# Second pass of a channel-attention kernel: a planner's order replaced by a written list of steps

## The chip, the cores and the metric

One NeuronCore of a Trainium2 chip. The metric is the device time of one execution in microseconds, the median of three runs. Engines are named as in the profile: PE (TensorE, matmuls), DVE (VectorE), ACT (ScalarE), POOL (GpSimd) and SP (SyncE, which here only issues transfers). Each engine takes its own instructions strictly in the order in which the program holds them.

## The reference

```python
def reference(x, w1d):                       # x: 1 x 384 x 384 x 384, bf16; w1d: 1
    B, H, W, C = x.shape
    g = jnp.einsum("bhwc->bc", x) / (H * W)  # mean of every channel
    s = jax.nn.sigmoid(g * w1d[0])
    return x * s[:, None, None, :]           # each channel scaled by its own factor
```

The input has 147,456 positions of 384 channels (113 MB). All of it must be read before the first element of the output is known.

## The kernel before

**Tiling.** The positions are split over the 128 partitions. One *row* below is one position on each of the 128 partitions: 384 bf16 values or 768 bytes in a partition. There are 1152 rows. The SBUF array `arena` holds 275 of them; `arena[:, a : a + n, :]` is n rows from place a.

**First pass.** All 1152 rows are loaded, and PE adds them up with a matrix of ones (line 246). ACT turns the sum into the factors `s_bf` (line 433) and copies these to a PSUM bank (`s_ps`, line 437). 784 rows are *streamed*: summed and dropped. The other 368 are *kept*, so that they need not be loaded again: 72 as they are (raw rows), 296 *folded*, that is, four rows' bits are squeezed into the space of three, in ten groups. Group 0 has 16 rows, groups 1 to 8 have 32, and group 9 has 24 and one more. Groups 0, 1, 3, 5, 7 stand one above the other in the arena from place 12 on (the left column), groups 2, 4, 6, 8 from place 140 on (the right column); group 9 (`BANKED`) waits in PSUM banks.

**Second pass.** Every row is multiplied by the factors and stored. `scale` (line 446) does one multiplication of n rows on DVE or on POOL; `scale_both` gives the last rows of a piece to POOL and the others to DVE. Raw rows are scaled and stored at once. A group is unfolded in five steps (`unfold_rows`): `fields`, `signs` and `three` are bit operations on DVE (lines 280 and 286) that rebuild the fourth row, `threefold` scales three quarters of the group, and `fourth` scales the rest. As places come free, the 784 streamed rows are loaded again (line 240), scaled and stored (line 473).

**What sets the order.** `Flow.add` records each step with what it reads and writes; `Flow.emit` writes the instructions out in the order in which they were recorded, and adds a semaphore wait wherever a step needs another engine's result, or the end of a transfer. All loads and stores are issued by SP and use one queue, q1. Transfers count on 24 semaphores in turn, `f_SP0` to `f_SP23`. A wait on SP holds every transfer that stands behind it.

The order of the second pass comes from a planner in the kernel, which runs when the program is built. It advances a clock in steps of 0.05 and keeps lists of what has landed (`landed`), is unfolding (`turns`), waits for its store (`waiting`) and is in the queue (`moves`). It takes a row as 0.2267 us of transfer (`ROW`), a scaling as 0.15 + 0.2 us a row (`TT`), and decides by thresholds that change at set times (`BIG`, `CAP`, `PART`, `LOW`, `LAST`, `MERGE`, `DEEP`, `SHORT`, `PENDING`) when to load how many rows, and when to scale, unfold or store. POOL gets a fifth of a piece of ten rows or more (`share`). The groups come in the order 7, 8, 5, 6, 9, 3, 4, 1, 2, 0.

Of the kernel before, what the change touches and what calls it, by code (L numbers as in the profile page):

```python
# [131 lines left out]
def kernel(  # L132
# [319 lines left out]
    beside = [False]  # L452

    def share(n):
        return n // 5 if beside[0] and n >= 10 else 0

    def scale_both(a, n):

        m = share(n)
        before = [s for s in fl.steps[-40:] if s.eng == "DVE"][-1:]  # L460
        scale(a, n - m, s=s_ps if beside[0] else s_bf)
        if m:
            scale(a + n - m, m, "POOL", after=before)

    THIN = {raw(A): (0, 12, 13)}

    def store(chunk, a, lo, hi):
        r0, n = chunk
        cuts = THIN[lo] if chunk == KEPT and lo in THIN else (0, hi - lo)
        for i, j in zip(cuts, cuts[1:]):  # L470
            step = fl.add(
                "SP",
                lambda i=i, j=j: nc.sync.dma_start(  # L473
                    out=view(of, r0, n)[:, lo + i : lo + j, :], in_=arena[:, a + i : a + j, :]
                ),
                reads=rows(a + i, j - i), dma=True,
            )
        return step
# [14 lines left out]
    def unfold_rows(a, at, p, n, more):  # L493
# [26 lines left out]
        def threefold():  # L520
            scale_both(a, 3 * n)

        def fourth():

            bits(u, u, XOR, FIX, AND, 0xFFFF, uc, uc)
            scale(at, n + more, s=s_ps if beside[0] else s_bf)

        return [
            (fields, lambda: 2 * TS(n) + TT(n)),
            (signs, lambda: 2 * TS(n) + TT(n)),  # L530
            (three, lambda: TS(3 * n) + TT(n)),
            (threefold, lambda: SC(3 * n)),
            (fourth, lambda: TS(n) + TT(n + more)),
        ]

    def TS(n):
        return 0.15 + 0.1 * n

    def SC(n):
        return TT(n - share(n))  # L540

    def TT(n):
        return 0.15 + 0.2 * n

# [50 lines left out]
    written = []  # L595


    ROW, PER_LOAD, PER_STORE = 0.2267, 0.112, 0.061
    LAT, SEEN, DT = 0.4, 1.5, 0.05
    PENDING, MERGE = 24.0, 12.0  # L600
    BIG, CAP, PART, LOW, LAST = 32, 48, 16, 9.0, 4.0
    DEEP, SHORT = 6.5, 1.0
    BESIDE = True
    BANKS_AT = 2
    N_SPLIT = 2
    now = dve_at = 0.0
    moves, waiting, over, acts = deque(), deque(), deque(), deque()
    landed = deque()
    idle = [False] * ROWS
    todo = 0  # L610
    last_is_load = False

    def release(a, n):
        for i in range(a, a + n):
            idle[i] = True

    def runs():
        got, i = [], 0
        while i < ROWS:
            if idle[i]:  # L620
                j = i
                while j < ROWS and idle[j]:
                    j += 1
                got.append((j - i, i))
                i = j
            else:
                i += 1
        return got

    def send(chunk, a, lo, hi, then, known=None):  # L630

        waiting.append((dve_at, hi - lo, then, chunk, a, lo, [] if known is None else known))

    def backlog():
        return sum(e[1] for e in moves) + ROW * sum(e[1] for e in waiting)

    def split(n, m):
        k = -(-n // m)
        cuts = [n * i // k for i in range(k + 1)]
        return list(zip(cuts, cuts[1:]))  # L640


    SCRATCH = rows(Y, 8)
    needed = [set(SCRATCH + rows(U, 8)), set(SCRATCH + rows(V, 8)), set(SCRATCH)]

    def stored(a, n):

        def f():
            for i in range(a, a + n):
                for left in needed:  # L650
                    left.discard(("a", i))
                if not Y <= i < Y + 8 and not U <= i < U + 8 and not V <= i < V + 8:
                    idle[i] = True
        return f


    landed.append((STREAMED, LAST_ROW, N_STREAM, 1, True))
    for a, n in (
        (Y + 5, 2), (Y + 2, 3), (T + 7, 3), (T + 4, 3), (T, 4), (A + 26, 6), (A + 32, 7), (A + 13, 13), (V + 4, 4), (A, 13)
    ):  # L660
        landed.append((KEPT, a, raw(a), n, True))


    alongside = deque()
    t = 1.0
    for a, n in ((U, 4), (U + 4, 4), (V, 4)):
        scale(a, n, "POOL", after=[copied])
        t += 0.2 + 0.84 * n
        alongside.append((t, KEPT, a, raw(a), n))


    order = [g for i in (3, 2) for g in (1 + 2 * i, 2 + 2 * i)] + [BANKED]
    order += [g for i in (1, 0) for g in (1 + 2 * i, 2 + 2 * i)] + [FIRST]
    line = deque(order)
    home = {g: i for i, column in enumerate(COLUMNS) for g in column}
    home[BANKED] = 2
    free = [True, True, True]
    total = len(GROUPS)
    out_rows = 0
    turns = deque()  # L680
    bank_at = None
    since = None
    asked = checked = False
    stall = 0.0

    def start_group():

        if not line:
            return False
        g = line[0]  # L690
        column = home[g]
        if needed[column] or not free[column] or g == BANKED and (bank_at is None or now < bank_at[1]):
            return False
        line.popleft()
        free[column] = False
        a, q = GROUPS[g]
        if g == BANKED:
            a = bank_at[0]

        below = 0  # L700
        if column < 2 and g != COLUMNS[column][0]:
            below = GROUPS[COLUMNS[column][COLUMNS[column].index(g) - 1]][1]

        def part():
            release(a + below, sent - below)

        def done():
            nonlocal out_rows
            out_rows += 1
            free[column] = True  # L710
            release(a + max(below, sent), n_rows - max(below, sent))

        turns.extend(step + (None,) for step in unfold(g, a))
        sent, n_rows = 0, 4 * q + (g == BANKED)
        if len(line) >= total - N_SPLIT and q == PAIR:

            f, t, _ = turns[-2]
            sent = 3 * q
            turns[-2] = (f, t, lambda: send(KEPT, a, c_group[g], c_group[g] + sent, part, written))
        f, t, _ = turns[-1]  # L720
        turns[-1] = (f, t, lambda: send(KEPT, a + sent, c_group[g] + sent, c_group[g] + n_rows, done, written))
        return True

    held, sent_off, loads = None, 0, 0
    BEHIND = {9: 2, 10: 1, 14: 1, 15: 1}
    while True:
        if now > 25:
            BIG, CAP, PART, LOW, LAST = 64, 48, 24, 9, 4
            MERGE, DEEP, SHORT, PENDING = 5, 4, 0.5, 14
        if now > 80:  # L730
            BIG, CAP, PART, LOW, LAST = 24, 56, 32, 9, 1
            MERGE, DEEP, SHORT, PENDING = 5, 14, 0.5, 30
        if now > 150:
            BIG, CAP, PART, LOW, LAST = 56, 85, 12, 4, 3
            MERGE, DEEP, SHORT, PENDING = 12, 2, 2, 14
        if now > 200:
            BIG, CAP, PART, LOW, LAST = 32, 72, 16, 2, 1
            MERGE, DEEP, SHORT, PENDING = 3, 20, 3, 40
        if dve_at <= now:
            ahead = backlog()  # L740
            can = bool(turns)
            if not can and not alongside and (ahead >= PENDING or not landed):
                can = start_group()
            if landed and (ahead < PENDING or not can):
                chunk, a, lo, n, end = landed.popleft()
                beside[0] = BESIDE and not alongside and bool(line or turns)
                if beside[0]:
                    scale_both(a, n)
                else:
                    scale(a, n, s=s_ps if alongside and now else s_bf)  # L750
                dve_at = now + SC(n)
                since = (a, lo) if since is None else since
                if end or ahead < MERGE:
                    b, first = since
                    send(chunk, b, first, lo + n, stored(b, lo + n - first))
                    since = None
            elif can:
                f, t, then = turns.popleft()
                beside[0] = BESIDE and not alongside
                f()  # L760
                dve_at = now + t()
                if then:
                    then()
# [10 lines left out]
        if not asked and not line and not turns:  # L774
            verdict()
            asked = True
# [85 lines left out]
```

## Time and profile before

| | us |
|---|---|
| median of 3 runs | 718.23 |
| lowest and highest run | 718.22, 718.54 |
| span of the profiled execution, first to last instruction | 715.5 |
| PE, DVE, ACT, POOL busy in it | 211.7, 467.4, 116.5, 98.1 |
| factors ready (`s_bf` written) | about 268.0 |
| first store issued, last store issued | 268.5, 688.3 |

The profile shows one execution. Its page has the busy time of every engine, the span in 40 slices of 17.9 us, and groups of instructions by line. A group's row reads: line, engine, operation, output<-input, sizes (partitions x elements), xcount | busy us, mean ns of one | idle time ahead of them and what ended it. 384 elements are one row, so `128x1536` is a piece of four rows. In the rows by stretches the columns are: from:to, length, busy us of PE, weight loads, DVE, ACT and POOL, then the granted share of the PE clock, the share of the 16 DMA engines that were busy, and GB/s. A share can go a little over 1.00, since a packet is counted where it starts.

### The profile page before, as it was taken

How to read it: one execution, taken by the hardware profiler on the slowest of the kernel's cores; microseconds unless marked ns; L12 is line 12 of the kernel's file. 1: busy time of each engine (PE TensorE's matmuls, PEld its weight loads, DVE VectorE, ACT ScalarE, POOL GpSimd, SP SyncE). 2: the span in 40 equal slices, each digit the busy share in tenths (PEclk: the TensorE clock that was granted, in tenths of full speed). 3: DMA queues.
4: the chain of work that ended last, by engine and by line, in shares of the span. 5: the costliest groups of instructions: out<-in, count | busy, mean ns of one | idle time of the engine just before them, and what ended most of it. 6: DMA issues, size and time to landing. Idle time of an engine off the chain costs nothing.

```text
span 715.5 us, 2029 instructions
## 1 busy us (share of the span) xinstructions
PE 211.7 (30%) x1202; PEld 0.3 (0%) x3; DVE 467.4 (65%) x383; ACT 116.5 (16%) x97; POOL 98.1 (14%) x46
## 2 busy tenths in 40 slices
PE   5667967999598680000000000000000000000000
PEld 0000000000000000000000000000000000000000
DVE  4600001799989849999999999999940597007840
ACT  3700001476667630000110000000000000000000
POOL 0000000000000005414233431167100000000000
PEclk9899998999899995555555555555555555555555
DMA  9999999999999989999999999999999999999997
GB/s 382 428 447 419 439 431 428 452 416 433 426 431 426 429 351 379 405 412 433 430 431 437 438 422 440 434 438 437 440 418 453 420 444 439 419 439 440 439 417 338
DMA packets 15996, 303.68 MB, mean 424 GB/s; under 512 B 1778, under 2 KB 2418, under 8 KB 5106
## 3 DMA queue, kind: packets, MB, share of 16 engines
q1 hardware_dynamic: 15984, 303.57, 99.1%
q8 instruction: 4, 0.07, 0.0%
q14 instruction: 6, 0.05, 0.0%
q10 hardware_dynamic: 2, 0.00, 0.0%
HBM read 190.32 MB, written 113.25 MB: 424 GB/s over the span
## 4 chain that ended last, share of the span: by engine, by line
DMA 48%; DVE 29%; PE 16%; ACT 1%; issue 1%; DVEq 0%; SPq 0%; another core or an unknown queue 0%; POOLq 0%
DMA arena<-in_x_dram 37%; DVE arena L446 20%; PE bank L246 16%; DMA out_dram<-arena 12%; DVE arena L280 5%; DVE arena L286 4%; ACT arena L317 1%; DVEq L107 0%; SPq L473 0%; SPq L240 0%; ACT s_bf L433 0%; SPq L113 0%; SPq L857 0%; POOLq L107 0%
## 5 line engine op out<-in xcount | busy, mean ns | idle before, releaser
L246 PE MATMUL bank<-arena,ones 128*128 128x384 bf16 x1151 | 203.6, 341 | 47.0 <-DMA arena<-in_x_dram 46.9
L280 DVE TENSOR_SCALAR arena<-arena 128x1536 uint16<-128x1536 uint16 (+2 forms) x199 | 140.4, 750 | 105.7 <-DMA arena<-in_x_dram 98.8
L446 POOL TENSOR_TENSOR arena<-arena,s_bf 128x768 bf16<-128x768 bf16 (+3 forms) x42 | 97.9, 2336 | 426.3 <-ACT bank L437 268.0
L446 DVE TENSOR_TENSOR arena<-arena,bank 128x3072 bf16<-128x3072 bf16 (+13 forms) x61 | 138.0, 2304 | 4.3 <-DMA arena<-in_x_dram 3.6
L446 DVE TENSOR_TENSOR arena<-arena,s_bf 128x5376 bf16<-128x5376 bf16 (+4 forms) x27 | 76.5, 2901 | 95.1 <-DMA arena<-in_x_dram 84.9
L286 DVE TENSOR_TENSOR arena<-arena 128x3072 uint16<-128x3072 uint16 (+2 forms) x90 | 117.6, 1307 | 13.5 <-PE bank L246 10.7
L317 ACT ACTIVATE arena<-arena 128x3072 uint16<-128x3072 uint16 (+1 forms) x38 | 102.4, 2696 | 146.0 <-DVE arena L280 146.0
L563 PE MATMUL bank<-odd,ones 128*128 128x1 bf16 x1 | 0.2, 185 | 259.4 <-DVE odd L558 259.4
L384 ACT COPY arena<-bank 128x512 uint32<-128x512 uint32 (+2 forms) x8 | 4.2, 533 | 87.3 <-DMA out_dram<-arena 87.2
L246 PE MATMUL bank<-s_bf,ones 128*128 128x384 bf16 x48 | 8.3, 326 | 0.0
L317 ACT ACTIVATION_READ_ACCUMULATOR arena<-arena 128x1 f32 x38 | 7.1, 186 | 0.0
L384 ACT COPY bank<-arena 128x512 uint32<-128x512 uint32 (+2 forms) x8 | 3.8, 528 | 0.0
L260 PE MATMUL bank<-arena,ones 128*128 128x384 bf16 x1 | 0.5, 477 | 6.8 <-DMA arena<-in_x_dram 6.8
L433 ACT ACTIVATE s_bf<-bank,w_sc 128x384 bf16<-128x384 f32 x1 | 0.6, 581 | 9.5 <-PE bank L246 9.5
L830 ACT ACT_TABLE_LOAD x1 | 1.3, 1283 | 0.7 <-PEq L846 0.7
L337 DVE MEMSET ones<- 128x128 bf16 x1 | 0.2, 165 | 1.1 <-PEq L846 1.1
L342 PE MATMUL bank<-w_bf,ones 1*128 1x1 bf16 x1 | 0.2, 182 | 2.1 <-DMA w_bf<-in_w1d_dram 2.1
L347 DVE TENSOR_SCALAR w_sc<-bank 128x1 f32<-128x1 f32 x1 | 0.2, 158 | 0.9 <-PE bank L342 0.9
L567 DVE CAST odd_i<-bank 128x1 int32<-128x1 f32 x1 | 0.2, 159 | 0.3 <-PE bank L563 0.3
L437 ACT COPY bank<-s_bf 128x192 uint32<-128x192 uint32 x1 | 0.3, 322 | 0.0
L563 PEld LDWEIGHTS bank<-odd,ones 128*128 128x128 bf16 x1 | 0.1, 103 | 517.7 <-DVE odd L558 517.7
L384 ACT COPY arena<-rest 128x64 uint32<-128x64 uint32 x1 | 0.2, 244 | 0.0
(10 smaller groups left out, 1.4 us busy)
## 6 DMA issues: line engine op xcount, KB each, us to landing
arena<-in_x_dram SPq DMA_DIRECT2D x3, 6912.0 KB, 36.2
out_dram<-arena SPq DMA_DIRECT2D x3, 6912.0 KB, 28.4
arena<-in_x_dram SPq DMA_DIRECT2D x4, 4608.0 KB, 24.5
arena<-in_x_dram SPq DMA_DIRECT2D x6, 3072.0 KB, 19.6
out_dram<-arena SPq DMA_DIRECT2D x6, 3072.0 KB, 21.6
arena<-in_x_dram SPq DMA_DIRECT2D x2, 6144.0 KB, 31.5
arena<-in_x_dram SPq DMA_DIRECT2D x2, 4992.0 KB, 23.1
arena<-in_x_dram SPq DMA_DIRECT2D x1, 8160.0 KB, 26.5
```

Of the source, the lines that this page charges most:

```text
L246: return pe.add_instruction(mybir.InstMatmult(name=nc.get_next_instruction_name(), ins=[pe.lower_ap(rhs), pe.lower_ap(ones[:])], outs=[pe. ...
L260: return nc.tensor.matmul(acc, lhsT=ones[:], rhs=arena[:, i, :], start=first, stop=last)
L280: lambda: nc.vector.tensor_scalar(out=dst, in0=src, scalar1=s0, scalar2=s1, op0=op0, op1=op1),
L286: "DVE", lambda: nc.vector.tensor_tensor(out=dst, in0=a, in1=b, op=op), reads=reads, writes=writes
L317: lambda: nc.scalar.activation(out=y, in_=y, func=ACTF.Copy, accum_out=seen[:, 2 * k + i : 2 * k + i + 1]),
L337: fl.add("DVE", lambda: nc.vector.memset(ones[:], 1.0), writes=["ones"])
L384: "ACT", lambda: nc.scalar.copy(dst.bitcast(u32), src.bitcast(u32)), reads=reads, writes=writes
L433: lambda: nc.scalar.activation(out=s_bf[:], in_=acc, func=ACTF.Sigmoid, scale=w_sc[:, 0:1]),
L437: "ACT", lambda: nc.scalar.copy(s_ps.bitcast(u32), s_bf[:].bitcast(u32)), reads=["s_bf"], writes=["bank0"]
L446: lambda: vec.tensor_tensor(out=v, in0=v, in1=s[:, None, :].to_broadcast([P, n, C]), op=Op.mult),
L563: lambda: nc.tensor.matmul(votes, lhsT=ones[:], rhs=odd[:], start=True, stop=True),
L830: nc.scalar.preload_act_table(ACTF.Sigmoid)
```

## The change

The planner with its clock, thresholds and lists is taken out. In its place stands `PLAN2`, a list of 164 entries, which a short loop turns into steps:

- `("M", a, n, m)`: scale n rows from place a, the last m of them on POOL
- `("U", g, a, m)`: the next unfolding step of group g, which stands at place a; in `threefold`, m rows go to POOL
- `("L", a, n)`: load the next n streamed rows to place a
- `("W", a, n)`: store n rows from place a
- `("B", a)`: bring group 9 back from the PSUM banks

The groups now come in the order 7, 5, 3, 8, 6, 1, 4, 2, 9, 0, and each piece has its own number of rows for POOL. The two passes' sums, the bit operations and the numbers of rows are the same. The diff, cut to its core:

```diff
-    def share(n):
-        return n // 5 if beside[0] and n >= 10 else 0
-
-    def scale_both(a, n):
-        m = share(n)
+    def scale_both(a, n, m):
         before = [s for s in fl.steps[-40:] if s.eng == "DVE"][-1:]
-        scale(a, n - m, s=s_ps if beside[0] else s_bf)
+        scale(a, n - m, s=s_ps if folded[0] else s_bf)
         if m:
             scale(a + n - m, m, "POOL", after=before)
...
-    def store(chunk, a, lo, hi):
+    def store(a, n):
+        chunk, lo = where[a]
...
-    ROW, PER_LOAD, PER_STORE = 0.2267, 0.112, 0.061
-    BIG, CAP, PART, LOW, LAST = 32, 48, 16, 9.0, 4.0
...
-    while True:
-        if now > 25:
-            BIG, CAP, PART, LOW, LAST = 64, 48, 24, 9, 4
...
+    PLAN2 = [
+        ("M", 274, 1, 0), ("M", 259, 4, 0), ("W", 274, 1), ("M", 269, 3, 0), ("W", 259, 4), ("M", 263, 3, 0),
...
+        ("U", 7, 84, 0), ("W", 246, 6), ("W", 232, 1), ("W", 216, 4), ("L", 252, 15), ("U", 7, 84, 0), ("L", 220, 32),
...
+    todo, turns = 0, {}
+    for kind, a, *more in PLAN2:
+        if kind == "M":
+            n, m = more
+            if a == LAST_ROW:
+                scale(a, n)
+            else:
+                scale_both(a, n, m)
+        elif kind == "W":
+            store(a, *more)
+        elif kind == "L":
+            (n,) = more
+            load(STREAMED, a, todo, todo + n)
...
+        else:
+            first, m = more
...
+            step = turns[a].popleft()
+            if step.__name__ == "threefold":
+                step(m)
+            else:
+                step()
```

In the rows below, a transfer is `DMA output<-input`, its size is partitions x elements, and the brackets name the semaphores that the instruction waits for: `f_DVE` and `f_POOL` count those engines' steps, `f_SP` and a number the end of a transfer.

SP at the start of the second pass, up to its first load. Before:

```order
L473 DMA out_dram<-arena 128x384 [waits f_DVE]
L473 DMA out_dram<-arena 128x768 [waits f_DVE]
L473 DMA out_dram<-arena 128x1152 [waits f_DVE] x3
L473 DMA out_dram<-arena 128x1536 [waits f_DVE]
L473 DMA out_dram<-arena 128x1536 [waits f_POOL]
```

Now:

```order
L467 DMA out_dram<-arena 128x384 [waits f_DVE]
L467 DMA out_dram<-arena 128x1536 [waits f_DVE]
L467 DMA out_dram<-arena 128x1152 [waits f_DVE] x2
L467 DMA out_dram<-arena 128x768 [waits f_DVE]
L467 DMA out_dram<-arena 128x1536 [waits f_POOL]
L467 DMA out_dram<-arena 128x2688 [waits f_DVE]
```

The second store has four rows instead of two.

SP around the first loads of the second pass. Before:

```order
L473 DMA out_dram<-arena 128x4608 [waits f_DVE]
L473 DMA out_dram<-arena 128x384
L240 DMA arena<-in_x_dram 128x8064 [waits f_SP23,f_SP0,f_SP22,f_SP2,f_SP3]
L240 DMA arena<-in_x_dram 128x4992 [waits f_SP5]
L240 DMA arena<-in_x_dram 128x4992 [waits f_SP8,f_SP9]
```

Now:

```order
L467 DMA out_dram<-arena 128x4608 [waits f_DVE]
L467 DMA out_dram<-arena 128x2304 [waits f_DVE,f_POOL]
L467 DMA out_dram<-arena 128x384 [waits f_DVE]
L467 DMA out_dram<-arena 128x1536 [waits f_DVE,f_POOL]
L240 DMA arena<-in_x_dram 128x5760 [waits f_SP22,f_SP20,f_SP1,f_SP2]
L240 DMA arena<-in_x_dram 128x12288 [waits f_SP6,f_SP4,f_SP7,f_SP8]
L467 DMA out_dram<-arena 128x5760 [waits f_DVE,f_POOL]
L467 DMA out_dram<-arena 128x9216 [waits f_DVE,f_POOL]
L467 DMA out_dram<-arena 128x3072 [waits f_DVE]
L240 DMA arena<-in_x_dram 128x4608 [waits f_SP12]
L467 DMA out_dram<-arena 128x12288 [waits f_DVE,f_POOL]
L467 DMA out_dram<-arena 128x4608 [waits f_DVE,f_POOL]
```

Loads of 15 and 32 rows stand in place of 21, 13 and 13. Two stores ahead of them now wait for POOL too, and a load of 12 rows with its store follows.

POOL at the start of the second pass, its first pieces. Before:

```order
L446 TENSOR_TENSOR arena<-arena,s_bf 128x1536 [waits f_ACT]
L446 TENSOR_TENSOR arena<-arena,s_bf 128x1536 x2
L446 TENSOR_TENSOR arena<-arena,s_bf 128x768 [waits f_DVE,f_SP10]
L446 TENSOR_TENSOR arena<-arena,s_bf 128x768 [waits f_DVE]
L446 TENSOR_TENSOR arena<-arena,s_bf 128x768 [waits f_DVE,f_SP11]
```

Now:

```order
L446 TENSOR_TENSOR arena<-arena,s_bf 128x1536 [waits f_ACT]
L446 TENSOR_TENSOR arena<-arena,s_bf 128x1536 x2
L446 TENSOR_TENSOR arena<-arena,s_bf 128x1152 [waits f_DVE]
L446 TENSOR_TENSOR arena<-arena,s_bf 128x768 [waits f_DVE]
L446 TENSOR_TENSOR arena<-arena,s_bf 128x1152 [waits f_DVE,f_SP10]
```

Pieces of three and two rows, which wait for DVE but for no load, stand ahead of the first piece that waits for a load.

264 lines of the change are left out of this document (40 added, 224 removed), and 26 rows, old and new, of the table PLAN2.

## The prediction

> **What bounds the kernel now.** I read the page's slices and DMA queues first, because they say in a few lines whether transfers ever pause.
>
> ```profile
> span 715.5 us, 2029 instructions
> PE 211.7 (30%) x1202; PEld 0.3 (0%) x3; DVE 467.4 (65%) x383; ACT 116.5 (16%) x97; POOL 98.1 (14%) x46
> ...
> DMA  9999999999999989999999999999999999999997
> ...
> q1 hardware_dynamic: 15984, 303.57, 99.1%
> ...
> HBM read 190.32 MB, written 113.25 MB: 424 GB/s over the span
> ```
>
> No compute engine passes 65%, while queue q1 (all of SP's transfers) keeps the 16 DMA engines at work for 99.1% of the span. Only slice 15 (from 250 us on) and the last one are below 9. The chain of waits gives VectorE 29% of the end, which misleads here: it follows semaphores, and a store that waits for a scaling may still find a long queue ahead of it. So I then asked for stretches of the second pass, which starts at 267.5 us, when the scale is ready.
>
> ```profile
> 266.00:270.00 4.00, 1.42 (x9) 0.00 (x0) 1.93 (x4) 0.90 (x2) 1.52 (x1) 1.00 0.14 49
> 270.00:285.00 15.00, 0.00 (x0) 0.00 (x0) 14.93 (x12) 0.00 (x0) 7.69 (x3) 0.51 1.02 416
> 285.00:290.00 5.00, 0.00 (x0) 0.00 (x0) 4.90 (x4) 0.00 (x0) 0.00 (x0) 0.50 1.03 364
> 290.00:295.00 5.00, 0.00 (x0) 0.00 (x0) 4.16 (x4) 0.00 (x0) 1.64 (x1) 0.50 0.97 413
> 295.00:300.00 5.00, 0.00 (x0) 0.00 (x0) 5.00 (x3) 0.00 (x0) 4.14 (x3) 0.50 1.00 387
> ...
> 315.00:320.00 5.00, 0.00 (x0) 0.00 (x0) 4.97 (x4) 0.00 (x0) 0.23 (x1) 0.50 0.97 372
> 320.00:530.00 210.00, 0.18 (x1) 0.10 (x1) 202.09 (x130) 4.41 (x9) 78.82 (x34) 0.50 1.01 434
> 530.00:710.00 180.00, 0.00 (x0) 0.00 (x0) 76.15 (x26) 0.00 (x0) 0.00 (x0) 0.50 1.00 434
> 710.00:716.00 6.00, 0.00 (x0) 0.00 (x0) 0.00 (x0) 0.00 (x0) 0.00 (x0) 0.50 0.17 73
> ```
>
> The last two columns are the share of the DMA engines and GB/s. From 270 to 710 us the share is 0.97 to 1.03: transfers never pause. The rate is 434 GB/s for 390 us and lower only early (364, 387, 372) though the share is full there: packets take longer, the queue isn't empty. VectorE is nearly as full until 527 us, but nothing is won by making it less so.
>
> A row of all 128 partitions is 128 x 768 B = 98,304 B, so at 434 GB/s it takes 0.2265 us. The second pass moves 784 rows in and 1152 out (bytes read, less the first pass's 1152 rows, plus bytes written: 190.3 MB), 438.5 us at that rate. From the first store's bytes (a little after 269 us) to about 711.5 us it takes 442. Some 3.7 us are all that a better order could recover; what it can lose is not bounded.
>
> **The change part by part.** The same code and the same order run up to the scale; 784 rows are still loaded and 1152 stored. What moves is the order behind 268 us, so I price four things: the head, the number of transfers, the places where the queue could run dry, and the slow early packets.
>
> *The head.* The first store (1 row) is as before. The second needs a scaling of 4 rows where it needed 2.
>
> ```profile
> L446 DVE TENSOR_TENSOR arena<-arena,bank 128x1536 bf16<-128x1536 bf16 x4 | 3.8, 951 | 0.1
> L446 DVE TENSOR_TENSOR arena<-arena,bank 128x1152 bf16<-128x1152 bf16 x4 | 2.8, 750 | 0.1
> L446 DVE TENSOR_TENSOR arena<-arena,bank 128x768 bf16<-128x768 bf16 x1 | 0.6, 555 | 0.0
> ...
> 269.00:270.00 1.00, 0.00 (x0) 0.00 (x0) 1.00 (x2) 0.00 (x0) 1.00 (x1) 1.00 0.42 146
> ```
>
> Before, the queue waits 0.555 - 0.23 = 0.33 us for the second store and 0.75 - 0.45 = 0.30 for the third. Now it waits 0.95 - 0.23 = 0.72 for the second and not at all for the third, 0.75 against 0.91 us of transfer. That is +0.1 us; bounds 0 and +0.4 (the whole 951 - 555 ns).
>
> *Number of transfers.* 46 stores replace 48, the loads stay 20. A transfer's own cost isn't shown; it lies between nothing and the 0.33 us that SP takes to issue one.
>
> ```profile
> L473 SPq DMA_DIRECT2D out_dram<-arena x48: 332/333/1252, 268.5 to 688.3; - x48
> ...
> DMA to landing us min/median/max: 1.6/15.7/39.6
> ```
>
> So 0 to -0.7 us. I take -0.1, near nothing: SP's issuing runs beside full transfers.
>
> *Cover.* The queue runs dry if a store or load reaches it after what is ahead has gone. SP issues in its order, so each wait also holds all that stand behind. I need VectorE's and GpSimd's durations:
>
> ```profile
> L446 POOL TENSOR_TENSOR arena<-arena,s_bf 128x1152 bf16<-128x1152 bf16 x2 | 4.7, 2370 | 2.4 <-DMA arena<-in_x_dram 2.4
> L446 POOL TENSOR_TENSOR arena<-arena,s_bf 128x768 bf16<-128x768 bf16 x22 | 36.0, 1640 | 50.3 <-DVE arena L286 26.7 <-DMA arena<-in_x_dram 15.5 <-DVE arena L446 7.9
> ...
> L286 DVE TENSOR_TENSOR arena<-arena 128x3072 uint16<-128x3072 uint16 x24 | 42.1, 1756 | 0.6
> L446 DVE TENSOR_TENSOR arena<-arena,bank 128x7680 bf16<-128x7680 bf16 x10 | 41.4, 4148 | 0.9 <-DMA arena<-in_x_dram 0.9
> L280 DVE TENSOR_SCALAR arena<-arena 128x3072 uint16<-128x3072 uint16 x40 | 37.5, 955 | 0.5
> ...
> L446 DVE TENSOR_TENSOR arena<-arena,bank 128x3072 bf16<-128x3072 bf16 x14 | 24.4, 1752 | 1.1 <-DMA arena<-in_x_dram 0.8
> L280 DVE TENSOR_SCALAR arena<-arena 128x9216 uint16<-128x9216 uint16 x8 | 20.5, 2559 | 0.2
> ```
>
> Scaling on VectorE costs (4.148 - 1.752) / 12 = 0.20 us a row and 0.15 fixed; unfolding steps one and two cost 2 x 0.955 + 1.756 = 3.67 us each, step three 2.56 + 1.76 = 4.3. A store's bytes follow its issue by about 1 us (first issue 268.5, bytes in 269 to 270), and I allow 2.5 us between the first DMA engine's end and the last one's (estimate: the share falls after 710 us while the span runs to 715.5).
>
> First place: both first loads stand behind a store that waits for GpSimd.
>
> ```profile
> 268.48 9.21 POOL L446 TENSOR_TENSOR arena<-arena,s_bf 128x1536 bf16<-128x1536 bf16 x3 [268.03 <-ACT bank L437]
> ...
> 268.07 12.70 DVE arena L446 x11
> ```
>
> GpSimd's three opening pieces end at 277.7 as before. VectorE's 12.70 us for 11 scalings of 59 rows become 10.3 for the 9 scalings of 48 rows up to the 12-row one, at 278.4. Then GpSimd's new pieces of 3 and 2 rows run to 278.4 + 2.37 + 1.64 = 282.4, SP issues the 4-row store, then the 15-row load, whose bytes can start at 283.9. Ahead of that store stand 67 rows, 269.3 + 0.7 + 15.2 = 285.2 us. It arrives at 283.4: 1.8 us of cover, cost nothing. Before, the first load was issued at 282.6 behind 74 rows; about the same.
>
> Second: the 12-row store behind the 12-row load. Behind that load stand 32 rows to store, 7.2 us. Spread 2.5, scaling of 10 rows 2.15, issue 1.0: 1.6 us are left.
>
> Third: the 19-row store, ahead of which VectorE does three unfolding steps of the next group (11.7 us) and scales 30 rows in three pieces (6.5), GpSimd then 3 rows (2.4); with the issue 21.6 us. When the 47-row load ahead of it is issued, 19 + 21 + 47 rows are queued, and a 32-row store follows: 27 us, less 2.5. Some 3 us are left, if VectorE starts that group when the load is issued.
>
> Later stores have transfers of 32 to 74 rows ahead (7 to 17 us). At the end the 74-row store has the 55-row load and the 47-row store ahead (23 us) against 15.1 us of scaling: 8, less 3.5. So starving costs 0, with bounds 0 and +4 (2.5 us more lag would overrun the first two places by some 1 us each, stores between them by as much).
>
> *The slow early packets.* Against 434 GB/s the stretches at 285, 295 and 315 us lose 0.81 + 0.54 + 0.71 = 2.06 us. They lie where small loads and stores alternate, and these are what the list rearranges: now 15 and 32 rows in, 15, 24 and 8 out, 12 in, 32 out, for 21, 13, 13 in and 10, 11, 13, 24 out. The profile doesn't name their cause. Bounds: none left, -2.06; twice as many, +2.06. I take the same loss: the alternation stays.
>
> Sum: 718.2 + 0.1 - 0.1 + 0 + 0 = 718.2 us. The profiled span is 715.5, the runs' median 718.23; the 2.7 us between are taken as they are.
>
> **A rule against it.** In the trace GpSimd's pieces ran beside VectorE's scalings from PSUM alone; while VectorE unfolds, GpSimd is idle (285 to 290 us: VectorE 4.90, GpSimd 0.00). Now the 3- and 2-row pieces run to 282.4 while unfolding starts at 280. The Trainium skill (SBUF — State Buffer, Who interferes with whom) says that a VectorE instruction in a 2-port mode, or with two SBUF inputs, and a GpSimd one exclude each other: the later fully blocks until the first is done. By that rule alone the 2-row piece could start one VectorE instruction late, at most 1.76 us by the row above, and the sum stays 718.2. No row here shows the two side by side.
>
> **Rivals.** *The early loss shrinks* (faster): with larger first transfers packets run at 434 GB/s, 718.2 - 2.06 = 716.2 at best; to be seen it must give back 1.4 of the 2.06. For it: those stretches alone are slow, and all small. Against: loads and stores still alternate there.
>
> *The cover is too thin* (slower): landings are seen, or VectorE is ready, some 2 to 3 us later than worked out; then the 12-row store, and the 15- and 24-row ones before it, reach an empty queue. From 1.6 us on, each us costs one, and at two or three places: +1.5 to +4, 720 to 722. For it: covers of 1.6 to 3 us on clocks carried over 15 to 110 us. Against: the present order has equally thin places (its first load), and shares of 0.97 and more.
>
> *GpSimd is kept out until unfolding pauses* (slower): its 2-row piece starts only after three steps, 280.0 + 11.7 = 291.7, ends at 293.3; store and loads reach a queue that emptied at 285.2, near 294.3: +9, 727 us. It decides from 1.8 us of delay. For it: nothing ran so before. Against: gaps between VectorE's instructions let GpSimd in.
>
> **How the numbers follow.** No change, early loss as now: 0.55, 718.2, own range 717.0 to 719.6. Early loss shrinks: 0.18, near 716.5. Thin cover: 0.19, near 721. GpSimd kept out: 0.08, 720 to 727. A difference is told from 0.2%, 1.44 us: faster below 716.8, 0.18; within, 0.55; slower above 719.7, 0.27. The range 716.3 to 721.8 leaves out GpSimd's bad case and some of both others.
>
> **What would show it.** Right: share 0.97 or more in every stretch from 271 to 710 us, first load issued near 283, GpSimd's 2-row piece ended near 282.5, 12-row store with bytes waiting ahead. Wrong: a dip of the share at 285, 298, 319 or 388 us; a GpSimd piece much over 0.73 us a row (2.37 for 3); or 285 to 320 us at 430 GB/s throughout (faster), or lower than now (slower).

## The result, and the profile after

The changed kernel takes 721.22 us (median of 7 runs, 719.93 to 722.74) against 718.28 us for the kernel before on the same chip (7 runs, 717.99 to 719.77). The ratio is 1.0037, 95% interval 1.0025 to 1.0048: slower, by 2.7 us. The forecast was no change, 718.2 us; the time lies inside its range, at the upper end, but above the 717.0 to 719.6 us that it gave to no change. The profiled execution took 721.69 us with a span of 719.5.

The page after, in the rows that answer to those of before:

```profile
PE 215.4 (30%) x1202; PEld 0.3 (0%) x3; DVE 475.3 (66%) x359; ACT 116.6 (16%) x97; POOL 90.1 (13%) x38
...
DMA  9999999999999989999999999999999999999997
...
q1 hardware_dynamic: 15696, 303.57, 98.9%
...
L280 DVE TENSOR_SCALAR arena<-arena 128x1536 uint16<-128x1536 uint16 (+2 forms) x199 | 147.8, 788 | 114.8 <-DMA arena<-in_x_dram 97.5
```

At this resolution nothing has happened: queue q1 is at 98.9% instead of 99.1%, and slices of 18 us average the loss away. One row is odd: the bit operations of line 280 have the same count and shapes as before and yet take 788 ns on average, where they took 750. The row before:

```profile
L280 DVE TENSOR_SCALAR arena<-arena 128x1536 uint16<-128x1536 uint16 (+2 forms) x199 | 140.4, 750 | 105.7 <-DMA arena<-in_x_dram 98.8
```

The loss shows in stretches of 5 to 25 us, whose last two columns are the share of the DMA engines that were busy and GB/s. After:

```profile
285.00:290.00 5.00, 0.00 (x0) 0.00 (x0) 4.90 (x4) 0.00 (x0) 0.00 (x0) 0.50 0.91 287
290.00:295.00 5.00, 0.00 (x0) 0.00 (x0) 4.82 (x4) 0.00 (x0) 0.44 (x1) 0.50 1.07 432
295.00:300.00 5.00, 0.00 (x0) 0.00 (x0) 5.00 (x2) 0.00 (x0) 4.78 (x2) 0.50 0.94 405
...
390.00:395.00 5.00, 0.00 (x0) 0.00 (x0) 4.97 (x3) 0.00 (x0) 1.25 (x2) 0.50 0.86 368
...
415.00:420.00 5.00, 0.00 (x0) 0.00 (x0) 4.93 (x4) 0.00 (x0) 0.00 (x0) 0.50 1.08 415
...
445.00:450.00 5.00, 0.00 (x0) 0.00 (x0) 5.00 (x2) 0.00 (x0) 2.37 (x1) 0.50 1.02 368
...
530.00:710.00 180.00, 0.18 (x1) 0.10 (x1) 113.85 (x58) 0.51 (x2) 13.48 (x6) 0.50 1.00 434
```

The same view of the kernel before, at the three later places:

```profile
390.00:395.00 5.00, 0.00 (x0) 0.00 (x0) 4.37 (x2) 0.00 (x0) 3.23 (x2) 0.50 1.02 437
415.00:420.00 5.00, 0.00 (x0) 0.00 (x0) 4.96 (x4) 0.00 (x0) 3.10 (x1) 0.50 0.99 428
445.00:450.00 5.00, 0.00 (x0) 0.00 (x0) 5.00 (x3) 0.00 (x0) 1.76 (x1) 0.50 1.02 437
```

Two kinds of loss are to be told apart. At 285 and 390 us the *share* falls (0.91, 0.86): the queue ran dry. At 415 and 445 us the share is full (1.08, 1.02) and only the *rate* is low (415 for 428, 368 for 437): there is work, but packets take longer. From 530 us on all is as before, 434 GB/s.

Rows of 5 us are rough: a packet is counted where it starts, and in the kernel before the share goes from 0.82 to 1.21 between 480 and 700 us though its engines are busy throughout. The trace also has a record of every packet, and two sums over these are used below, in us for each of the 16 DMA engines. *Idle time* is time without a packet. *Slow packets* are the time of each packet above the shortest of its size in these profiles. Idle time is 0.75 us from 280 to 300 us and 0.47 from 380 to 400, against 0.08 and 0.02 before.

The sums account for the loss. From its first packet to its last, the second pass of these two executions takes 448.0 us for 444.5. Of the 3.5 us, 2.2 are slow packets (4.9 us for 2.7; 1.6 for 0.1 of them from 390 to 460 us), 1.5 are idle time, and 0.3 came back because there are fewer packets.

The timeline of the changed kernel (start, duration, engine, line; the number in brackets is idle time and what ended it) shows what came late, at the first place and at the third:

```profile
279.06 4.67 POOL L446 TENSOR_TENSOR arena<-arena,s_bf 128x1152 bf16<-128x1152 bf16 x2 [0.82 <-DVE arena L446]
280.29 4.25 DVE L280 TENSOR_SCALAR arena<-arena 128x3072 uint16<-128x3072 uint16 x2
284.51 2.66 SPq L240 DMA_DIRECT2D arena<-in_x_dram  x2
...
366.24 0.33 SPq L240 DMA_DIRECT2D arena<-in_x_dram  x1
368.41 1.82 DVE L280 TENSOR_SCALAR arena<-arena 128x3072 uint16<-128x3072 uint16 x2
...
375.95 2.36 POOL L446 TENSOR_TENSOR arena<-arena,s_bf 128x1152 bf16<-128x1152 bf16 x1 [11.01 <-DVE arena L280]
376.39 4.34 DVE L280 TENSOR_SCALAR arena<-arena 128x9216 uint16<-128x9216 uint16 x1
...
390.40 0.34 SPq L467 DMA_DIRECT2D out_dram<-arena  x1
```

At both places a GpSimd piece runs beside a bit operation, and the bit operation stretches: two 8-row operations take 4.25 us at 280.29 and 1.82 at 368.41, where GpSimd is idle; the 24-row operation takes 4.34 where it took 2.56 before. At the third place SP issues the 19-row store only at 390.40. In the trace's records of transfers, the 32-row store ahead of it was through on the first of the 16 DMA engines at 390.45 and on the last at 393.30; the new store's packets begin at 391.25, and until then the faster engines had nothing to do. The time from the first to the last of the 16 engines to finish one transfer, 2.85 us here, is called the *lag* below.

### The profile page after: what moved, and what is told of

It reads as the page before. It is cut to its first block, busy times and chain, and to the rows that moved or that the text cites. A ratio compares the mean times of both kernels' runs of the same rounds, so it can differ in the third digit from the quotient of the medians.

```text
span 719.5 us, 1992 instructions
## 1 busy us (share of the span) xinstructions
PE 215.4 (30%) x1202; PEld 0.3 (0%) x3; DVE 475.3 (66%) x359; ACT 116.6 (16%) x97; POOL 90.1 (13%) x38
## 3 DMA queue, kind: packets, MB, share of 16 engines
q1 hardware_dynamic: 15696, 303.57, 98.9%
## 4 chain that ended last, share of the span: by engine, by line
DMA 50%; DVE 28%; PE 15%; ACT 2%; DVEq 1%; POOL 1%; issue 1%; SPq 0%; POOLq 0%
DMA arena<-in_x_dram 37%; DVE arena L446 16%; PE bank L246 15%; DMA out_dram<-arena 12%; DVE arena L280 7%; DVE arena L286 5%; ACT arena L317 2%; DVEq L107 1%; POOL arena L446 1%; SPq L240 0%; SPq L467 0%; ACT s_bf L433 0%; SPq L113 0%; SPq L683 0%; POOLq L107 0%
## 5 line engine op out<-in xcount | busy, mean ns | idle before, releaser
L280 DVE TENSOR_SCALAR arena<-arena 128x1536 uint16<-128x1536 uint16 (+2 forms) x199 | 147.8, 788 | 114.8 <-DMA arena<-in_x_dram 97.5
L246 PE MATMUL bank<-arena,ones 128*128 128x384 bf16 x1151 | 207.5, 345 | 43.7 <-DMA arena<-in_x_dram 43.5
L446 DVE TENSOR_TENSOR arena<-arena,bank 128x3072 bf16<-128x3072 bf16 (+24 forms) x54 | 155.2, 2912 | 27.2 <-DMA arena<-in_x_dram 26.7
L446 POOL TENSOR_TENSOR arena<-arena,s_bf 128x1536 bf16<-128x1536 bf16 (+6 forms) x34 | 89.9, 2648 | 492.3 <-ACT bank L437 268.6
L446 DVE TENSOR_TENSOR arena<-arena,s_bf 128x9984 bf16<-128x9984 bf16 (+7 forms) x10 | 59.4, 5994 | 57.5 <-DMA arena<-in_x_dram 46.8
L260 PE MATMUL bank<-arena,ones 128*128 128x384 bf16 x1 | 0.5, 477 | 6.9 <-DMA arena<-in_x_dram 6.9
```

Source lines behind the costliest of these rows:

```text
L246: return pe.add_instruction(mybir.InstMatmult(name=nc.get_next_instruction_name(), ins=[pe.lower_ap(rhs), pe.lower_ap(ones[:])], outs=[pe. ...
L260: return nc.tensor.matmul(acc, lhsT=ones[:], rhs=arena[:, i, :], start=first, stop=last)
L280: lambda: nc.vector.tensor_scalar(out=dst, in0=src, scalar1=s0, scalar2=s1, op0=op0, op1=op1),
L446: lambda: vec.tensor_tensor(out=v, in0=v, in1=s[:, None, :].to_broadcast([P, n, C]), op=Op.mult),
```

## The experiments

The measured times below stand beside a run of the kernel before on the same chip; "ratio" is against that. All edits are to the list `PLAN2` of the changed kernel, but for one. The questions in order: is it the stretched bit operations, is it the first pieces, is it the addresses, is it the dry queue at 390 us, and what do 415 and 445 us have to do with that?

**The kernel before, unchanged (c_before).**

> The kernel before, unchanged, as a measure of what runs of one kernel differ by: ratio 1.000 within 0.002. Its profile shows how much of the second pass's length (444.5 us in the first profile, 448.0 in the changed kernel's) is the order's own: within 0.7 us of 444.5 if the slow packets belong to the order, up to 447 if they come and go by chance.

718.45 us (12 runs), ratio 0.9999, 0.9989 to 1.0009. Its second pass takes 445.0 us for 444.5 and has 2.4 us of slow packets for 2.7, so these belong to the order. A ratio of 1.001 can't be told from 1 here, one of 1.002 can.

**No GpSimd piece beside the first unfolding (e1_start).** The pieces of 3 and 2 rows go to VectorE:

```diff
-("M", 246, 6, 3), ("W", 220, 12), ("M", 232, 1, 0), ("M", 216, 4, 2),
+("M", 246, 6, 0), ("W", 220, 12), ("M", 232, 1, 0), ("M", 216, 4, 0),
```

> The two GpSimd pieces of 3 and 2 rows that ran to 283.7 us beside unfolding are given to VectorE. Theory lock (GpSimd and VectorE's unfolding hold each other up, so the 4-row store and the first loads came late): the two bit operations at 280 us take 1.9 us again instead of 4.25, the first load is issued at about 282.5 instead of 284.5, the share at 285 to 290 us is 1.00 instead of 0.91, and about 1.0 us is won against the changed kernel: near 720.2. Theory size (the slow packets belong to the small transfers and loads of 15 and 32 rows, whoever scales): share 1.00 but the rate at 285 to 290 stays under 370 GB/s, win 0.5 at most: 720.7.

Its timeline, and its stretch at 285 us:

```profile
280.58 1.82 DVE L280 TENSOR_SCALAR arena<-arena 128x3072 uint16<-128x3072 uint16 x2
...
283.16 3.42 SPq L240 DMA_DIRECT2D arena<-in_x_dram  x2
```

```profile
285.00:290.00 5.00, 0.00 (x0) 0.00 (x0) 4.90 (x4) 0.00 (x0) 0.00 (x0) 0.50 1.00 367
```

The lock is confirmed: the two bit operations take 1.82 us instead of 4.25. The first load is issued 1.35 us earlier, though 0.70 of that is only an earlier start of this execution's second pass (first store at 268.30 for 269.00). Idle time from 280 to 300 us falls from 0.75 to 0.24. The rate stays at 367 GB/s, as the size theory had it. The whole time doesn't move: 721.17 us, ratio 1.0044 (1.0022 to 1.0065). The gap at 285 us is real, and no gain from closing it can be seen; in this profile the idle time at 380 to 400 us is 1.28 us for 0.47, which hides half a microsecond.

**No GpSimd piece beside the unfolding at 376 us (e2_mid), and beside none at all (e3_all).**

```diff
-("M", 68, 6, 3),
+("M", 68, 6, 0),
```

> The 3-row GpSimd piece at 376 us, which ran beside a bit operation of 24 rows (4.34 us instead of 2.56), goes to VectorE. Theory lock: the 19-row store is issued some 1.2 us earlier than at 390.4 (1.8 less 0.6 for three more rows), the share at 390 to 395 us rises from 0.86 to 0.95 or more, and if a queue that runs dry brings the 16 DMA engines into step and makes packets slow afterwards (theory step), the slow stretches at 415 and 445 us go too: 1.5 to 2 us won, 719.5. Theory size: the stretches at 415 and 445 stay at 415 and 368 GB/s, 0.4 won, 720.8.

720.77 us, ratio 1.0033 (1.0018 to 1.0048). The bit operation is back at 2.55 us, but three rows more on VectorE take 0.6 us, and the 19-row store comes 22.95 us behind the 47-row load instead of 24.16. (All of this execution's second pass runs some 1.6 us later.) The store was issued at 391.59, the first DMA engine was through at 392.24: still too late. The slow packets at the next two changes stayed, 0.60 and 1.03 us.

For e3_all the edits of e1_start and e2_mid are made together, and GpSimd's share of group 9 falls from 4 and 3 rows to 2 and none.

> All GpSimd pieces that ran beside bit operations are taken from GpSimd (280, 376, 564 and 572 us). Theory lock with step: no dip of the share after 271 us, no slow stretch after 320 us, 718.3 to 718.8, the kernel before within 0.1%. Theory lock alone: dips go, slow stretches stay, 720. Theory size: 720.5 to 721.

721.23 us, ratio 1.0041 (1.0025 to 1.0058). The 19-row store was issued at 389.46, and the first engine was through at 389.86, so the queue ran dry here too, against the expectation (0.54 us of idle time from 380 to 400 us). Taking the mutual stretching away gives VectorE its time back, but by itself it brings the kernel nothing.

**A smaller second piece (e4_head).**

```diff
-("M", 259, 4, 0), ("W", 274, 1), ("M", 269, 3, 0), ("W", 259, 4),
+("M", 259, 2, 0), ("W", 274, 1), ("M", 261, 2, 0), ("W", 259, 2), ("M", 269, 3, 0), ("W", 261, 2),
```

> The second piece of 4 rows is cut into two of 2 rows, each with its own store. The prediction's head term: 0.1 us back, 721.1. The trace of the changed kernel shows more, 0.45 us more idle queue at 270 to 280 us than before, so up to 0.5 us back, 720.7, if the head is worth its idle time. Everything else as in the changed kernel: share 0.91 at 285 and 0.86 at 390.

720.86 us (6 runs), ratio 1.0045 (1.0028 to 1.0061): nothing gained. Its profiled execution was its fastest (719.12 us), and is of use for another reason. In it the lag was 1.0 us, so SP saw them complete earlier and issued the 19-row store at 387.86, 2.0 us before the first engine was through. There was no dip, and its stretch from 390 to 460 us is at 433 GB/s. So the third place is decided by some 2 us of lag, and the lag of one kernel varies: it is 2.5 and 3.3 us in the two profiles of the kernel before.

**Other addresses (e5_rows).** The streamed rows are read again from the other end:

```diff
-            load(STREAMED, a, todo, todo + n)
+            at = N_STREAM - todo - n
+            load(STREAMED, a, at, at + n)
```

> Order, sizes and places in SBUF as in the changed kernel, but the streamed rows are read and written from the other end of their chunk, so each transfer meets other addresses in HBM. Theory address (packets slow where the addresses read and those being written fall badly together): the slow stretches at 417 and 447 us (0.6 and 0.9 us summed over engines, in all four profiles with this order where the queue ran dry at 390) go or move elsewhere. Theory turn (packets slow at a change between loading and storing, wherever the rows lie): they stay at 415 to 452. Time 720 to 722 by both, less by up to 1.5 if they go and none come.

721.83 us, ratio 1.0051 (1.0036 to 1.0067), with the slow stretches where they were (390 to 460 us at 421 GB/s; slow packets of 0.65 and 0.87 us at the two changes). Other addresses don't move them.

**The 19-row store in time (e6_s19), twice (c_s19).** Rows 68 to 87 are scaled and stored before the third unfolding step of group 8 instead of after it, without GpSimd:

```diff
-("U", 8, 188, 0), ("W", 36, 32), ("U", 8, 188, 0), ("M", 68, 6, 3), ("U", 8, 188, 0), ("U", 8, 188, 3),
-("M", 74, 6, 0), ("M", 80, 7, 3), ("M", 87, 21, 1), ("W", 68, 19), ("U", 8, 188, 0), ("W", 87, 21),
+("U", 8, 188, 0), ("W", 36, 32), ("U", 8, 188, 0), ("M", 68, 6, 0), ("M", 74, 6, 0), ("M", 80, 7, 0),
+("W", 68, 19), ("U", 8, 188, 0), ("M", 87, 21, 1), ("W", 87, 21), ("U", 8, 188, 3), ("U", 8, 188, 0),
```

> The 19 rows are scaled and stored before the third unfolding step of group 8, the 21 rows before its fourth, with no GpSimd share in the 19. The 19-row store is issued near 380 us instead of 390.4, the share at 390 to 395 is 1.0 instead of 0.86. Theory step (a queue that runs dry brings the 16 engines into step, and packets slow at the next turns): the slow stretches at 417 and 447 shrink to under 0.5 us together, and 1.5 to 2 us are won: 719.2. Theories address and turn: they stay, 0.4 us won: 720.8.

> The kernel of e6_s19 unchanged, as the control for the next two: both theories expect what it gave, 1.0016 of the kernel before (1.0005 to 1.0028), no dip of the DMA engines' share at 390 us, and shares of 0.98 or more from 415 to 420 and 445 to 450 us at over 425 GB/s.

719.30 and 719.68 us (12 runs each), ratios 1.0016 (1.0005 to 1.0028) and 1.0018 (1.0009 to 1.0027): about 1.4 us of the 2.7 are back, with intervals that just touch the changed kernel's (1.0025 to 1.0048). The store is issued at 379.43, and all three later places recover at once, although nothing was changed at 415 and 445 us. e6_s19 by stretches:

```profile
390.00:395.00 5.00, 0.00 (x0) 0.00 (x0) 4.97 (x4) 0.00 (x0) 0.38 (x2) 0.50 1.00 426
415.00:420.00 5.00, 0.00 (x0) 0.00 (x0) 4.93 (x4) 0.00 (x0) 0.00 (x0) 0.50 1.08 469
445.00:450.00 5.00, 0.00 (x0) 0.00 (x0) 5.00 (x2) 0.00 (x0) 2.37 (x1) 0.50 0.97 418
```

These are places where the queue passes from stores to loads (416 to 420 us) and from loads to stores (447 to 452). The step theory says why one dry spell could slow them: it brings the 16 DMA engines into step, and engines that turn together hinder one another. Stretches of half a microsecond show that they do fall into step. After:

```profile
410.00:410.50 0.50, 0.00 (x0) 0.00 (x0) 0.50 (x1) 0.00 (x0) 0.00 (x0) 0.50 2.00 866
410.50:411.00 0.50, 0.00 (x0) 0.00 (x0) 0.50 (x2) 0.00 (x0) 0.00 (x0) 0.50 0.50 217
411.00:411.50 0.50, 0.00 (x0) 0.00 (x0) 0.50 (x1) 0.00 (x0) 0.00 (x0) 0.50 0.17 72
411.50:412.00 0.50, 0.00 (x0) 0.00 (x0) 0.47 (x2) 0.00 (x0) 0.00 (x0) 0.50 2.34 1011
```

And e6_s19:

```profile
410.00:410.50 0.50, 0.00 (x0) 0.00 (x0) 0.50 (x2) 0.00 (x0) 0.00 (x0) 0.50 0.67 289
410.50:411.00 0.50, 0.00 (x0) 0.00 (x0) 0.50 (x1) 0.00 (x0) 0.00 (x0) 0.50 1.50 650
411.00:411.50 0.50, 0.00 (x0) 0.00 (x0) 0.47 (x2) 0.00 (x0) 0.00 (x0) 0.50 0.67 289
411.50:412.00 0.50, 0.00 (x0) 0.00 (x0) 0.50 (x1) 0.00 (x0) 0.00 (x0) 0.50 0.67 289
```

A packet is counted where it starts. After the dry spell hardly any of the 16 engines starts one from 411.0 to 411.5, and most of them do in the next half microsecond (0.17, then 2.34); where the queue never ran dry the starts are spread more evenly (0.67 to 1.50). In all five kernels whose queue ran dry at 390 us (after, e1_start, e2_mid, e3_all, e5_rows), 9 to 14 of the 16 engines finish the 32-row store near 408 us within 0.2 us of one another; in the others it is 4 to 7.

The step doesn't explain the cost, though. Near 450 us, at the second change, 6 engines are that close in the changed kernel and 6 in e6_s19, and the change costs 0.84 us in the one and 0.02 in the other. In e9_turns below, 9 are that close at 488 us, and the change there costs 0.01. So the step is seen, and it is not shown to be the cause.

**A dry spell at another place (e8_dip).** This tests whether a dry spell by itself slows the changes behind it, as the step theory foretells. From e6_s19, the third step of group 1 goes ahead of the scalings for the 64-row store:

```diff
-("U", 1, 12, 0), ("M", 44, 32, 4), ("U", 1, 12, 0), ("M", 76, 32, 3), ("M", 196, 24, 4),
-("W", 44, 64), ("M", 220, 47, 6), ("W", 196, 24), ("U", 1, 12, 4), ("W", 220, 47),
+("U", 1, 12, 0), ("U", 1, 12, 0), ("U", 1, 12, 4), ("M", 44, 32, 4), ("M", 76, 32, 3), ("M", 196, 24, 4),
+("W", 44, 64), ("M", 220, 47, 6), ("W", 196, 24), ("W", 220, 47),
```

> From e6_s19, one wait made longer at another place: the third step of group 1 is put ahead of the scalings for the 64-row store, so that this store, issued at 451.2 us, 3.2 us before the first of the 16 engines was through with what stood ahead, is issued about 4.2 us later and the queue runs dry for the first engines near 455 us. Step theory (a queue that runs dry brings the 16 engines into step, and packets are then slow where loads take over from stores and stores from loads): besides the dip itself, 0.5 to 1 us, slow stretches at the next two such places, near 493 and 525 us, 0.4 to 0.9 us each; in all 1.3 to 2.8 us over c_s19. Rival (the dip costs only its own idle time, and what went at 417 and 447 us had another cause): 434 GB/s at 493 and 525 us, and 0.5 to 1 us over c_s19.

721.87 us, ratio 1.0050 (1.0037 to 1.0064), against 1.0018 for c_s19 on the same chip: 2.3 us. The store is issued at 457.05, the first engine had been through with the one ahead at 456.41, the last at 459.55. (This execution's second pass starts 1.9 us later than that of c_s19.) By stretches, e8_dip and then c_s19:

```profile
415.00:420.00 5.00, 0.00 (x0) 0.00 (x0) 4.90 (x4) 0.00 (x0) 0.00 (x0) 0.50 1.01 438
...
490.00:495.00 5.00, 0.00 (x0) 0.00 (x0) 0.86 (x1) 0.00 (x0) 0.00 (x0) 0.50 0.98 413
...
525.00:530.00 5.00, 0.00 (x0) 0.00 (x0) 2.08 (x1) 0.00 (x0) 0.13 (x1) 0.50 0.88 314
```

```profile
415.00:420.00 5.00, 0.00 (x0) 0.00 (x0) 4.90 (x4) 0.00 (x0) 0.00 (x0) 0.50 1.02 441
...
490.00:495.00 5.00, 0.00 (x0) 0.00 (x0) 0.30 (x1) 0.00 (x0) 0.00 (x0) 0.50 1.13 486
...
525.00:530.00 5.00, 0.00 (x0) 0.00 (x0) 2.10 (x2) 0.00 (x0) 0.93 (x1) 0.50 1.02 439
```

415 us stays fast, and now the next two changes between loads and stores are slow, 413 and 314 GB/s for 486 and 439 in these rough rows. Packet by packet the changes at 497 and 530 us cost 0.72 and 0.78 us here, and 0.02 and 0.04 in c_s19; the rival's price, the dry spell alone, is exceeded. The spell itself is 1.06 us of idle time, and 1.06 + 0.72 + 0.78 = 2.6 us stand against the 2.3 measured. In the changed kernel the changes at 419 and 451 us cost 0.62 and 0.84, in e6_s19 0.00 and 0.02; with the spell's 0.47 that is 1.9 us, for the 1.4 that e6_s19 gave back.

**All repairs together (e7_fix).** e6_s19 with the edits of e1_start, e4_head and group 9.

> Both places mended at once, and the head: the second piece cut in two, no GpSimd pieces beside unfolding at 280, 564 and 572 us, the 19 and 21 rows scaled earlier. If the idle queue (0.2 at the head, 0.65 at 280 to 300, 0.5 at 380 to 400 us more than before) is the loss: 719.7 with the slow packets left. If the slow packets follow from it: 718.3 to 718.8.

719.79 us, ratio 1.0019 (1.0008 to 1.0029): no better than e6_s19 alone, and not the 718.3 to 718.8 expected if the slow packets all followed from the idle queue.

**Fewer changes between loads and stores early (e9_turns).** From e6_s19:

```diff
-("W", 108, 8), ("L", 252, 12), ("M", 236, 16, 2), ("W", 220, 32), ("U", 5, 60, 0),
-("M", 252, 12, 2), ("U", 5, 60, 0), ("W", 252, 12), ("L", 92, 24), ("U", 5, 60, 0), ("L", 220, 32),
-("L", 252, 15), ("U", 5, 60, 4),
+("W", 108, 8), ("M", 236, 16, 0), ("W", 220, 32), ("L", 252, 12), ("U", 5, 60, 0),
+("L", 92, 24), ("U", 5, 60, 0), ("L", 220, 32), ("M", 252, 12, 2), ("W", 252, 12), ("U", 5, 60, 0),
+("U", 5, 60, 4),
...
-("L", 148, 52)
+("L", 148, 67)
```

> From e6_s19, fewer places early where loads and stores take over from each other: the 12-row load goes behind the next 32-row store, the second 15-row load is dropped and its rows are added to the 52-row load near the end (67 rows). Between 285 and 345 us loads and stores then change over 4 times instead of 6, the number of rows stays. Turn theory (the early packets are slow at these changes, some 0.5 us each): 1 us less, 717.5 to 718.8 us. Rival (the loss belongs to the start of the mixed traffic, however often it turns): the same slow packets in fewer places, as c_s19.

720.87 us, ratio 1.0033 (1.0022 to 1.0045): slower than c_s19, where a gain was expected.

```profile
300.00:310.00 10.00, 0.00 (x0) 0.00 (x0) 9.23 (x5) 0.00 (x0) 0.12 (x1) 0.50 0.91 388
...
315.00:320.00 5.00, 0.00 (x0) 0.00 (x0) 2.62 (x2) 0.00 (x0) 0.00 (x0) 0.50 0.92 337
```

The 12-row load had been cover for the 32-row store behind it: that store was now issued at 309.29, the first engine was through with the 8-row store ahead at 309.23. The next two changes, at 318 and 335 us, cost 0.67 and 1.11 us. This is no further proof, since changes this early are slow without a dry spell too: c_s19 pays 1.0 us at the change near 340 us, and the slow packets from 285 to 345 us sum to 3.1 us in both. What e9_turns has on top is the spell itself, 0.8 us of idle time, and 0.6 us more of slow packets from 345 to 470 us. Whether fewer changes by themselves would help was not tested by it.

**All together.** Rates from the stretches of each profiled execution, GB/s; the dry spell is in bold:

| | ratio | 285 to 345 us | 345 to 390 | 390 to 460 | 460 to 535 | 535 to 705 |
|---|---|---|---|---|---|---|
| before, c_before | 1, 0.9999 | 415, 418 | 433, 433 | 435, 436 | 432, 431 | 435, 435 |
| after | 1.0037 | 412 | 431 | **427** | 428 | 434 |
| e1_start | 1.0044 | 415 | **424** | **424** | 432 | 433 |
| e2_mid | 1.0033 | 410 | 432 | **424** | 430 | 435 |
| e3_all | 1.0041 | 414 | **425** | **424** | 433 | 433 |
| e5_rows | 1.0051 | 413 | 432 | **421** | 432 | 433 |
| e6_s19, c_s19 | 1.0016, 1.0018 | 413, 409 | 432, 432 | 436, 435 | 432, 432 | 434, 434 |
| e7_fix | 1.0019 | 411 | 432 | 435 | 432 | 433 |
| e8_dip | 1.0050 | 415 | 432 | 431 | **420** | 434 |
| e9_turns | 1.0033 | **403** | 429 | 434 | 434 | 432 |

In every kernel of the table whose queue ran dry behind 300 us the ratio is 1.0033 or more, in every one without it 1.0019 or less. (e4_head is left out, since its profiled execution is not like its other runs.) A stretch of 70 us at 427 instead of 435.5 GB/s is 70 x 8.5 / 434 = 1.4 us, what e6_s19 gave back.

## Why the prediction was wrong, step by step

**What bounds the kernel** was right: queue q1 does, and every loss found is one of the queue's. **The head** is of the size forecast. Summed over the 16 engines' packets, idle time up to 280 us is 0.46 us a DMA engine instead of 0.27: +0.2 for the +0.1 forecast, inside its bounds. **Number of transfers**: 66 transfers make 9504 packets in the second pass instead of 9792, and the sum of their shortest times is 0.3 us smaller, for the 0.1 forecast and inside its bounds.

**First place**: 1.8 us of cover were forecast, with the first load issued near 283. It was issued at 284.51. Of the delay, 0.5 us is a later start of this execution's second pass (first store at 269.00 for 268.46). Most of the rest is what the rule against the change named, in a stronger form. GpSimd's two pieces ended 1.3 us later than worked out (279.06 + 4.67 = 283.7, the 0.5 included), but the real loser was VectorE, 4.25 - 1.82 = 2.4 us. The Trainium skill (SBUF — State Buffer, Who interferes with whom) says that the two exclude each other, and the trace agrees: 4.25, and 4.34 for 2.56 at 376 us. I had let GpSimd alone pay. GpSimd's 4.67 us for 5 rows, 0.93 a row, is one of the signs of being wrong that the prediction named, and the dips at 285 and 390 us are two more.

Yet the cover as the sum defined it held: the queue ahead also took longer than worked out. The 4-row store was issued at 283.75, its bytes were due at 284.75, and the store ahead was through on the first engine only at 286.63, 1.9 us later. The share fell behind that store, at the load. The microsecond from issue to bytes had been read from a store; here fifteen engines were through with the store ahead 2.9 us after the load's issue at the latest, but six began the load at 2.8 us and the other ten only at 3.4 to 5.0. In the kernel before the first load is issued 4.9 us before the store ahead is through, and the idle time from 280 to 300 us is 0.08; with 4.0 us it is 0.24 (e1_start), with 3.1 us 0.75 (after). Why a load starts so late here isn't known. In the whole time this place was worth too little to be seen (e1_start).

**Second place**: right. The 12-row store was issued at 318.48, and the 32-row store ahead was through at 320.88 on the first engine; less the microsecond to the bytes, 1.4 us of cover for 1.6.

**Third place**: this is the step that failed: "Some 3 us are left, if VectorE starts that group when the load is issued." VectorE started it at 368.41, 2.2 us after the load, because the last step of group 3 came first; and the 24-row bit operation was stretched by 1.8 us. The sum of durations was good: 390.40 - 368.41 - 1.8 = 20.2 us for the 20.6 worked out without the issue. So was the queue's side: from the load's issue to the first engine through, 390.45 - 366.24 = 24.2 us for 27 less 2.5. So 3 became 3 - 2.2 - 1.8 + 0.4 = -0.6 (measured: bytes from 391.25 on for a queue that emptied from 390.45 on, -0.8), and the queue ran dry. The "if" was left standing as a condition, though the list answers it: the last step of group 3 stands ahead of group 8's first.

**Starving cost 0** failed with it, and not only in size. The *thin cover* rival named the 12-, 15- and 24-row stores at one microsecond of time for each one of lateness. Lateness came at the 19-row store, which it had not named, and most of what that cost came later, at two changes between loads and stores 28 and 60 us on, where the queue was full (0.62 + 0.84 us, for 0.47 of idle time at 390 us). e6_s19 takes all three away with one edit, and e8_dip makes them anew at another place. That the rival's time, near 721, is the one measured is in good part luck: its places were others, and its price left out the larger half.

**The slow early packets** were taken as unchanged. The 2.06 read from rates was right: packet by packet, 285 to 345 us cost 2.1 and 1.8 us in the two profiles of the kernel before. After, they cost 2.5, and 2.1 to 3.1 in the other kernels with the list, so a term that stood at 0 was about +0.5, with a scatter as large. The faster rival is out, and *GpSimd kept out until unfolding pauses* is too: its pieces ran at once.

**Left open.** e6_s19 is still 0.16% slower than before, 1.2 us. The packets say where it goes, and not why. In e6_s19, c_s19 and e7_fix the slow packets from 285 to 345 us cost 2.5, 3.1 and 3.1 us, 0.4 to 1.3 more than before, and the idle time up to 300 us is 0.65, 0.45 and 0.15 us more; together that is about all of the rest. e7_fix mends the head, the first pieces and GpSimd, and has more slow packets in place of the idle time. That a dry spell makes the next two changes between loads and stores slow is shown; how it does so isn't, by the engines' step or otherwise. No version faster than the kernel before came out of this.

## What to carry to other kernels

Where a full queue sets the time, cover is to be computed from the moment at which the *last* engine lets the previous transfer be seen complete to the moment at which the *first* engine runs out, with everything that the list puts ahead on the computing engine; a cover of 3 us over a 24 us sum was none here. A load is to be issued earlier than a store: 3 us ahead of its need was too late here, 4.9 us was not. A short dry spell costs more than its own length, since the next changes between loads and stores go slowly too: look for a dip ahead of low rates at a full share (here 28 to 73 us ahead) before looking for a cause at those places. A GpSimd scaling beside VectorE's bit operations took its time from VectorE.

## What the runs showed of the hardware

- In one queue over 16 DMA engines, a transfer lands on the last engine 1.0 us (e4_head) to 4.5 us (e3_all) after the first at the same place of nearly the same program, and this lag stays for hundreds of microseconds (2.5 us from 317 to 712 us in the kernel before).
- After a dry spell of 0.3 to 1.3 us of idle time the next two changes between loads and stores cost 0.60 to 0.74 and 0.78 to 1.03 us of slow packets: near 419 and 451 us in five kernels, at 497 and 530 in e8_dip. The third change in those five costs 0.00 to 0.03. Without a spell the two at 419 and 451 cost 0.00 to 0.03 in e6_s19, c_s19 and e7_fix, and 0.04 and 0.41 in e4_head. The lag doesn't decide: at the first of them it is 0.6 us in e4_head, which loses 0.04, and 3.1 us in e3_all, which loses 0.74.
- A store that finds idle engines starts on the first ten of them 0.85 to 1.0 us after its issue (19-row store of the changed kernel). The first load of the second pass starts on the last engine 4.3 to 5.0 us after its issue in ten of the eleven profiles of kernels with the list (e4_head's records don't tell), and engines wait for it there (0.15 to 0.75 us of idle time from 280 to 300 us).
- VectorE's bit operations and GpSimd's multiplication exclude each other in large part: 4.34 us for 2.56 beside a GpSimd piece of 2.36 us; GpSimd's 3- and 2-row pieces at 279.06 took 4.67 for 2.37 + 1.64.
